# Wide rows for wo of heads 12 and 13, b1 in 16 rows, w2 in four pieces, early clearing of semaphores and sixteen more matmuls in a decode attention kernel

## The chip, the cores and the metric

The kernel runs on one core of a Trainium2 chip. The metric is the device time of one launch in microseconds. TensorE (PE) does matmuls into PSUM, VectorE (DVE) and ScalarE (ACT) do the rest of the arithmetic, GpSimd (POOL) makes one identity matrix, and SyncE (SP) issues almost all transfers. Transfers that SP issues stand in one queue that 16 transfer engines work off in order; ACT has a queue of its own for a few small loads and half of the stores.

## The reference

```
def _A_ref(x, k_cache, v_cache, wq, wo):            # B=2, H=16, Sk=4096, Dh=256, D=448
    q = (x @ wq).reshape(B, Sq, H, Dh).transpose(0, 2, 1, 3)
    scores = einsum("bhqd,bhkd->bhqk", q, k_cache) * (Dh ** -0.5)
    o = einsum("bhqk,bhkd->bhqd", softmax(scores), v_cache)
    return o.transpose(0, 2, 1, 3).reshape(B, Sq, H * Dh) @ wo
def _B_ref(x, w1, b1, w2, b2):                      # F=1792
    h = einsum("bsd,df->bsf", x, w1) + b1
    r = where(h > 0, h, 0)
    return einsum("bsf,fd->bsd", r * r, w2) + b2
g = sigmoid((x * gate_w).sum(-1, keepdims=True))
return g * A + (1 - g) * B                          # [2, 1, 448] float32
```

One query per batch row attends over 4096 cached keys; K and V are 134 MB each in float32, so nearly all of the kernel is reading them once.

## The kernel before

The work goes in 16 rounds (`rounds`): round i is one batch row and two heads. A round's K is 8192 KB, two heads on the 128 partitions, 64 partitions for each head, and so is its V. K goes by turns into the buffers `kp[0]` and `kp[1]`; V goes into `vp`, that of round 14 into `kp[0]`. DVE multiplies half a K by q (L412) and sums each row (L417), twice a round; PE turns the maxima over partitions (`maximum`, L427), ACT takes the exponentials (`softmax`, L435), and PE multiplies them with V (`values`, L479). A matmul is two PE instructions in float32, and four matmuls of different column groups run side by side.

Rounds 0 to 11 run on PE as a loop, the rest is written out. Heads are grouped in units: three of four heads (0 to 11), then 12, 13 and 14, 15. After each wide unit `turn_wide` turns the result so that it can be multiplied with wo, and `project` (L539) adds it to the sum `acc`. For the two last units `turn_narrow` (L518) and `late_wo` (L547) do the same on PSUM `fin`, four column quarters at a time; `late_w2` (L563) adds the second product of the feed-forward part to the same `fin`.

wo of a wide unit is loaded so that partition p holds 8 successive rows of wo, 14,336 bytes in one piece (`wo_g`, L531). For the last four heads it is loaded head by head, 3,584 bytes for each partition and head (`wo_v`, L530, in `load_wo`, L533). w2 goes into the first 6272 columns of `kp[1]` in five pieces with the borders `W2_CUTS` (L198), the V of the last round in three pieces with the borders `V_CUTS`.

Nothing plans the order: every engine does its operations in the order in which the code calls them, and waits on semaphores that `Flow` (L24) works out from what each reads and writes. On SP the last issues are: V of round 14, wo, the three pieces of V of round 15 (they wait for PE to be done with `vp`), five pieces of w2 (they wait for DVE to have summed the first half of `kp[1]`), a store of the unfinished result, and the last store. `store` (L638) writes half of the output from SP and half from ACT. At the end SP waits for both stores and then clears all semaphores (L171 to L174).

At the start ACT issues x, gate_w, b2 and b1; b1 goes straight into its final layout, 128 partitions with 14 numbers each (L305). It is used once, in `ffn_square` (L579). PE multiplies x with wq (L398), then with w1.

Of the kernel before, what the change touches and what calls it, by code (L numbers as in the profile page):

```python
# [6 lines left out]
AF = mybir.ActivationFunctionType  # L7
ALU = mybir.AluOpType
# [15 lines left out]
class Flow:  # L24
# [7 lines left out]
    def __init__(self, nc):  # L32
        self.nc = nc
        self.eng = {PE: nc.tensor, ACT: nc.scalar, DVE: nc.vector, POOL: nc.gpsimd, SP: nc.sync}
        self.order = {e: [] for e in self.eng}
        self.ops = {}
        self.know = {e: {} for e in self.eng}
        self.seen = {}
        self.tokens = {}
        self.parts, self.part, self.at = None, None, 0  # L40

    @staticmethod
    def span(r):
# [77 lines left out]
    def emit(self):  # L121
        nc = self.nc
        sems = {}
        counts = {}
        for proc, ops in self.ops.items():
            at = 0
            for o in ops:
                if proc not in self.eng:
                    o.inc = not o.give
                if o.inc and not o.give:  # L130
                    at += 1 if proc in self.eng else 16
                counts[id(o)] = at
        assert all(not t for t in self.tokens.values())

        def sem(name):
            if name not in sems:
                sems[name] = nc.alloc_semaphore(f"s_{name}")
            return sems[name]

        for proc in self.ops:  # L140
            sem(proc)
        for t in self.tokens:
            sem(t)

        def one(o):
# [12 lines left out]
        for eng in (POOL, DVE, ACT, SP, PE):  # L158
            for o in self.order[eng]:
                if isinstance(o, Op):  # L160
                    one(o)
                else:
                    outer, inner, body, rest, slot = o
                    engines = bass.OrderedEngineSet([TYPES[PE]])
                    with nc.Fori(0, outer, engines=engines, head_slot={TYPES[PE]: slot}):
                        with nc.Fori(0, inner, engines=engines):
                            for p in body:
                                one(p)
                        for p in rest:
                            one(p)  # L170
            if eng == SP:  # L171
                nums = sorted(s.num for s in sems.values())
                assert nums == list(range(nums[0], nums[0] + len(nums)))
                nc.sync.sem_clear(range(nums[0], nums[0] + len(nums)))  # L174


def gated_mix_kernel(nc, x, k_cache, v_cache, wq, wo, w1, b1, w2, b2, gate_w, out):
# [32 lines left out]
    def sb(name, *shape):  # L210
        return nc.alloc_sbuf_tensor(name, shape, F32).ap()
# [12 lines left out]
    rs_t = [sb(f"rs{n}", P, B * HG) for n in range(2)]  # L224
    eo = sb("eo", P, 2)
    m16 = sb("m16", P, 4 * HG)
    m8 = sb("m8", P, 2 * HG)
    rw = sb("rw", P, 2 * HG)
    o_t = sb("o", P, DH)
# [19 lines left out]
    oTn = [sb(f"oTn{n}", P, NJ, 2 * B) for n in range(2)]  # L249

    po_t = [bank(f"po{n}") for n in range(2)]
    acc = bank("acc")
# [9 lines left out]
    def load(eng, sem, dst, src, w, r=(), give=None):  # L262
        e = flow.eng[eng]
        op(eng, lambda: e.dma_start(dst, src), r=r, w=w, dma=sem, give=give)  # L264
# [32 lines left out]
    def at_start(k, n=1):  # L297
        return place(kp[1], k * D, (k + n) * D)
# [17 lines left out]
    def vec(fn, r, w, give=None):  # L316
        op(DVE, fn, r=r, w=w, give=give)
# [11 lines left out]
    vec(lambda: v_.tensor_reduce(m16, ident.rearrange("p (r k) -> p k r", r=4)[:, :4 * HG, :], axis=AX.X, op=ALU.add),  # L329
        ["ident"], ["m16"])  # L330
    vec(lambda: v_.tensor_reduce(m8, m16.rearrange("p (c s) -> p c s", s=2), axis=AX.X, op=ALU.add), ["m16"], ["m8"])

    xr = start_at[:, 4 * D:].rearrange("b (k r s) -> b k r s", k=XC, s=2)
    for s in range(2):
# [6 lines left out]
    def mms(calls):  # L341
        def run():
            for out_, lhsT, rhs, start, stop in calls:
                i = t_.matmul(out_, lhsT, rhs, start=start, stop=stop, skip_group_check=True)  # L344
            return i
        return run
# [158 lines left out]
    def turn_wide(u):  # L505
# [7 lines left out]
        for k in range(HG):  # L513
            at = slice(k * HP, (k + 1) * HP)
            op(ACT, lambda k=k, at=at: s_.activation(oTw[at], ptv[at, :, B * k:B * k + B], AF.Copy), r=["sm"], w=[("oTw", k, k + 1)],
               give="oT" if k == HG - 1 else None)

    def turn_narrow(u, between=lambda: None):  # L518
        ptv = sm[:, :NJ * 2 * B].rearrange("p (j c) -> p j c", c=2 * B)
        a = u - NG + 1  # L520
        po, name, rl, oT = po_t[u % 2], f"po{u % 2}", rl_t[u % 2], oTn[a]
        o = shared[:, a * 512:(a + 1) * 512]
        op(ACT, lambda: s_.activation(o, po, AF.Copy), r=[name], w=[("shared", a * 512, (a + 1) * 512)])  # L523
        between()
        ov = o.rearrange("r (s p j) -> r s j p", s=2, j=NJ)
        op(PE, mms([(ptv[:, j, :], ov[:, s, j, :], rl[:, :2 * B, s], s == 0, s == 1) for j in range(NJ) for s in range(2)]),
           r=[("shared", a * 512, (a + 1) * 512), f"rl{u % 2}"], w=["sm"])
        op(ACT, lambda: s_.activation(oT, ptv, AF.Copy), r=["sm"], w=[f"oTn{a}"])  # L528

    wo_v = wo.rearrange("(h p j) n -> p h (j n)", p=P, j=NJ)  # L530
    wo_g = wo.rearrange("(g p j) n -> g p (j n)", p=P, j=HJ)  # L531

    def load_wo(u):  # L533
# [12 lines left out]

    def late_wo(h):  # L547
        u, k = unit_of[h]
        t = wo_t.rearrange("p (h j n) -> p h j n", h=HG, j=NJ)
        calls = []  # L550
        for j in range(NJ):
            calls += late(oTn[u - NG + 1][:, j, B * k:B * k + B], t[:, h % HG, j, :])
        op(PE, mms(calls), r=[f"oTn{u - NG + 1}", "wo"], w=["fin"])
# [97 lines left out]
    softmax(i + 1)  # L651
    times_q(i + 2, 0, LEAD, J)
    values(i, vt)
    turn_narrow(NG - 1)
# [28 lines left out]
    vec(lambda: v_.tensor_copy(y4, fin[:, :DQ]), ["fin"], [("shared", 0, DQ)])  # L683
    store(y4, ("shared", 0, DQ))
    op(SP, lambda: nc.sync.nop(), r=["out0", "out1"])
    flow.emit()


# [24 lines left out]
```

## Time and profile before

| | us |
|---|---|
| median of 3 runs (lowest, highest) | 678.0 (677.81, 679.03) |
| the profiled execution's own time | 677.88 |
| its span, first to last instruction | 676.6 |
| PE, DVE, ACT busy | 259.4, 577.0, 49.5 |
| HBM read | 289.56 MB |
| mean granted TensorE clock | 0.649 |

The span is cut into 40 slices of 16.9 us in the page's timeline; a digit is a busy share in tenths. In the chain of waits a row is start, time and what the chain ran on; in the timeline it is start, time, engine, line and operation, with the idle time before it and what ended that in brackets. A row of issues ends with the time from issue to landing.

### The profile page before, as it was taken

Reading aid. Unit: us, or ns where it says so; the run is one execution under the profiler, and the core shown is the slowest. Engines: PE = TensorE matmul, PEld = TensorE weight load, DVE = VectorE, ACT = ScalarE, POOL = GpSimd, SP = SyncE. Lnnn points to the kernel's source line nnn. Section 1 sums busy time; section 2 is a strip of 40 time slices with the busy share of each in tenths; the row PEclk is TensorE's granted clock in tenths of the full one; section 3 lists DMA queues with packets and bytes.
Section 4 is the critical chain, followed back from the end, with each engine's and each line's share of the span. In section 5 each row is a group of like instructions: output and inputs, shape, how many; then the busy total and the mean of one; then the engine's idle time right before and its main releaser. Section 6 shows DMA issues by size and latency. Waiting matters only on the chain.

```text
span 676.6 us, 3524 instructions
## 1 busy us (share of the span) xinstructions
PE 259.4 (38%) x1518; PEld 84.0 (12%) x1518; DVE 577.0 (85%) x166; ACT 49.5 (7%) x151; POOL 0.7 (0%) x6
## 2 busy tenths in 40 slices
PE   2622151512305662150515356051421563512487
PEld 1100010100101310010101311010100133100123
DVE  3069999999999896989989896998989899999940
ACT  0100101010000301010010301001010120000000
POOL 0000000000000000000000000000000000000000
PEclk9957585655658576585756577575665775575888
DMA  9999999999999999999999999999999999999997
GB/s 381 434 430 435 434 434 434 434 434 434 434 434 434 446 434 434 434 430 430 434 434 426 457 434 434 434 434 434 434 430 434 396 465 430 434 434 434 390 437 292
DMA packets 7059, 289.66 MB, mean 428 GB/s; under 512 B 902, under 2 KB 1036, under 8 KB 1932
## 3 DMA queue, kind: packets, MB, share of 16 engines
q1 hardware_dynamic: 6880, 289.54, 99.2%
q8 instruction: 5, 0.08, 0.0%
q10 hardware_dynamic: 172, 0.02, 0.0%
q14 instruction: 2, 0.02, 0.0%
HBM read 289.56 MB, written 0.01 MB: 428 GB/s over the span
## 4 chain that ended last, share of the span: by engine, by line
DMA 42%; DVE 26%; PE 4%; issue 0%; ACT 0%; SPq 0%
DMA kp<-in_A_k_cache_dram 26%; DMA vp<-in_A_v_cache_dram 16%; DVE s L417 13%; DVE kp L412 13%; PE po L344 4%; PE fin L344 0%; PE sm L344 0%; PE mt L344 0%; SPq L264 0%; ACT shared L523 0%; DVE nb L440 0%; DVE shared L683 0%; ACT oTn L528 0%
## 5 line engine op out<-in xcount | busy, mean ns | idle before, releaser
L412 DVE TENSOR_TENSOR kp<-kp,q 128x8192 f32<-128x8192 f32 (+2 forms) x34 | 278.3, 8184 | 48.1 <-DMA kp<-in_A_k_cache_dram 47.9
L417 DVE TENSOR_REDUCE s<-kp 128x32 f32<-128x8192 f32 x32 | 277.9, 8686 | 1.1
L344 PE MATMUL po<-vp,pw 128*16 128x512 f32 (+1 forms) x960 | 141.1, 753 | 216.1 <-PEq L148 195.9
L344 PEld LDWEIGHTS po<-vp,pw 128*16 128x16 f32 (+1 forms) x960 | 32.1, 113 | 328.9 <-issue 307.2
L344 PE MATMUL mt<-ident,m 128*128 128x128 f32 x32 | 11.8, 468 | 139.9 <-PEq L148 90.5
L459 ACT ACTIVATE pw<-zero 128x128 f32<-128x128 f32 x12 | 3.7, 312 | 317.1 <-PE po L344 317.1
L344 PEld LDWEIGHTS mt<-ident,m 128*128 128x128 f32 x32 | 7.6, 295 | 153.3 <-issue 101.2
L344 PE MATMUL acc<-wo,oTw 128*2 128x448 f32 x48 | 25.2, 694 | 3.2 <-PEq L148 3.2
L448 ACT ACTIVATE pw<-s,nb 64x64 f32<-64x64 f32 x32 | 11.1, 348 | 193.5 <-DVE nb L440 193.3
L344 PE MATMUL pq<-qs,sel 128*128 128x512 f32 x24 | 22.4, 1036 | 0.0
L440 DVE TENSOR_REDUCE nb<-mt 64x1 f32<-64x64 f32 x32 | 7.1, 221 | 13.1 <-PE mt L344 12.6
L683 DVE COPY shared<-fin 128x112 f32<-128x112 f32 x1 | 0.3, 275 | 19.9 <-PE fin L344 19.9
L344 PE MATMUL sm<-rw,shared 128*128 128x8 f32 x48 | 10.7, 360 | 11.5 <-PEq L148 11.5
L392 ACT ACTIVATE q<-pq 64x256 f32<-64x256 f32 x32 | 12.1, 379 | 24.8 <-PE pq L344 24.5
L344 PE MATMUL ph<-vp,xT 128*4 128x448 f32 x28 | 8.3, 765 | 14.2 <-DMA vp<-in_B_w_dram 14.2
L344 PE MATMUL po<-kp,pw 128*8 128x512 f32 x64 | 9.6, 754 | 8.7 <-DMA kp<-in_A_v_cache_dram 8.7
L344 PEld LDWEIGHTS sm<-rw,shared 128*128 128x128 f32 x48 | 10.5, 330 | 11.7 <-issue 11.7
L344 PE MATMUL po<-vp,xT 128*4 128x512 f32 x56 | 8.8, 798 | 4.7 <-DMA vp<-in_A_wq_dram 4.7
L344 PE MATMUL sm<-ident,wo 4*128 4x4 f32 x28 | 7.0, 380 | 1.9 <-ACT wo L572 1.9
L344 PEld LDWEIGHTS acc<-wo,oTw 128*2 128x2 f32 x48 | 4.6, 100 | 21.6 <-issue 21.6
L344 PEld LDWEIGHTS sm<-ident,wo 4*128 4x128 f32 x28 | 6.9, 336 | 2.8 <-ACT wo L572 2.8
L507 ACT ACTIVATE shared<-o 128x1024 f32<-128x1024 f32 x3 | 6.3, 2101 | 2.6 <-DVE o L503 2.6
(76 smaller groups left out, 79.6 us busy)
## 6 DMA issues: line engine op xcount, KB each, us to landing
vp<-in_A_wq_dram SPq DMA_DIRECT2D x1, 7168.0 KB, 19.4
wo<-in_A_wo_dram SPq DMA_DIRECT2D x4, 1792.0 KB, 44.6
vp<-in_A_v_cache_dram SPq DMA_DIRECT2D x1, 4096.0 KB, 24.7
vp<-in_B_w_dram SPq DMA_DIRECT2D x1, 3136.0 KB, 17.9
vp<-in_A_v_cache_dram SPq DMA_DIRECT2D x1, 3072.0 KB, 31.6
kp<-in_B_w_dram SPq DMA_DIRECT2D x1, 1344.0 KB, 37.1
vp<-in_A_v_cache_dram SPq DMA_DIRECT2D x1, 1024.0 KB, 33.7
kp<-in_B_w_dram SPq DMA_DIRECT2D x2, 448.0 KB, 33.5
```

The source lines that it names most:

```text
L344: i = t_.matmul(out_, lhsT, rhs, start=start, stop=stop, skip_group_check=True)
L392: op(ACT, lambda k=k, at=at: s_.activation(t[at], pq[at, k * DH:(k + 1) * DH], AF.Copy), r=["pq"], w=[(f"q{i % 3}", k, k + 1)])
L412: vec(lambda: v_.tensor_tensor(kt, kt, q.unsqueeze(1).to_broadcast([P, hi - lo, DH]), op=ALU.mult), at + [f"q{i % 3}"], at)
L417: vec(lambda: v_.tensor_reduce(s[:, at], rows(t)[:, at, :], axis=AX.X, op=ALU.add), [place(t, half * HALF, (half + 1) * HALF)], [(f"s{i % ...
L440: vec(lambda at=at: v_.tensor_reduce(nb[at], mt[at, at], axis=AX.X, op=ALU.max, negate=True), ["mt"], [(f"nb{i % 2}", at.start, at.stop)])
L448: op(ACT, lambda: s_.activation(pw[at, :, 2 * c:2 * c + 2], s[at].rearrange("p (m s) -> p m s", s=2), AF.Exp, bias=nb[at], accum_out=rs[at ...
L459: op(ACT, lambda: s_.activation(at, zero.unsqueeze(2).unsqueeze(3).to_broadcast([P, NK // 2, 2, 2]), AF.Copy), r=["zero"], w=[("pw0", 2 * ...
L507: op(ACT, lambda: s_.activation(o_w, o_t.rearrange("r (p j) -> r j p", j=HJ).unsqueeze(2).to_broadcast([P, HJ, HG, HP]), AF.Copy), r=["o"] ...
L683: vec(lambda: v_.tensor_copy(y4, fin[:, :DQ]), ["fin"], [("shared", 0, DQ)])
```

## The change

- **wo of heads 12 to 15.** `load_wo(NG - 1)` loads heads 12 and 13 alone, in wide rows, into partitions 0 to 63 of the wo tile. `turn_half` is new: it turns unit 3 as `turn_wide` turns the wide ones, two ACT copies, 16 matmuls, two ACT copies into `oT2` of 64 partitions; `late_half` multiplies with 32 matmuls. `load_wo(NG)` loads heads 14 and 15 in the old rows, into free columns of `kp[1]` behind w2; `late_wo` reads them there.
- **b1.** It is loaded as 16 rows of 112 numbers. A matmul with a 16-row selection matrix `e16` spreads each row to 8 partitions, a multiplication with the mask `m_i` and a sum pick the 14 numbers of each partition. All of it lies in `kp[1]` before K of round 1 is loaded there.
- **w2.** The pieces 0 to 2 and 2 to 8 become one.
- **Order on PE.** The first two chunks of w2 are no longer multiplied during the last turn, but after it with the rest.
- **Matmuls in waits.** `keep_busy` multiplies a matrix of ones with data that lie in `kp[0]`, into PSUM `ph`, which nobody reads any more: 6 before the first piece of the last V, 10 after it.
- **Semaphores.** ACT reports when it has issued its last store; SP then clears all semaphores but those of the two stores, waits for these, and sets each back by subtraction.

```diff
-    W2_CUTS = (2, 8, 11, 13)
+    W2_CUTS = (8, 11, 13)
+    BUSY = (6, 10)
...
-    load(ACT, "b1", b1T, b1.rearrange("(p c) -> p c", c=FC), ["b1T"])
+    load(ACT, "b1", b1r, b1.rearrange("(r n) -> r n", r=BR), [b1r_at])
...
+    op(PE, mms([(ph[:, :BI * FC], e16, b1r, True, True)]), r=[e16_at, b1r_at], w=["ph"])
+    vec(lambda: v_.tensor_tensor(b1w.rearrange("p (c i) -> p c i", i=BI), ph[:, :BI * FC].rearrange("p (i c) -> p c i", i=BI),
+                                 m_i.unsqueeze(1).to_broadcast([P, FC, BI]), op=ALU.mult), ["ph", "m_i"], [b1w_at])
+    vec(lambda: v_.tensor_reduce(b1T, b1w.rearrange("p (c i) -> p c i", i=BI), axis=AX.X, op=ALU.add), [b1w_at], ["b1T"])
...
+    def turn_half():
+        u = NG - 1
+        ptv = sm[:PH, :HJ * 2 * B].rearrange("p (j c) -> p j c", c=2 * B)
...
+        op(PE, mms([(ptv[:, j, :], ov[:, s, j, :], rl[:, :2 * B, s], s == 0, s == 1) for j in range(HJ) for s in range(2)]),
+           r=["shared", f"rl{u % 2}"], w=["sm"])
...
+        elif u < NG:
+            load(SP, "wo", wo_t[:PH], wo_g[u, :PH], ["wo"])
         else:
-            load(SP, "wo", wo_t.rearrange("p (h k) -> p h k", h=HG), wo_v[:, u * HG:(u + 1) * HG, :], ["wo"])
+            load(SP, "wo_e", wo_e.rearrange("p h j n -> p h (j n)"), wo_v[:, H - 2:, :], [wo_e_at])
...
+    def keep_busy(n):
+        op(PE, mms([(ph[32 * (k % 4):32 * (k % 4) + 16, :], ones_pp[:, :16], kp[0][:, :2 * DH], True, True) for k in range(n)]),
+           r=["ones", place(kp[0], 0, 2 * DH)], w=["ph"])
...
+    def late_half():
+        t = wo_t[:PH].rearrange("p (j n) -> p j n", j=HJ)
+        calls = []
+        for j in range(HJ):
+            calls += late(oT2[:, j, :], t[:, j, :])
+        op(PE, mms(calls), r=["oT2", "wo"], w=["fin"])
...
     load_wo(NG - 1)
+    load_wo(NG)
     vt_next = load_v(i + 1, vp, V_CUTS)
...
-    late_wo(H - 4)
-    late_wo(H - 3)
+    late_half()
     sums(NG)
     norm(NG)
+    keep_busy(BUSY[0])
...
         values(last, vt, lo, hi)
-    turn_narrow(NG, lambda: late_w2(0, W2_CUTS[0]))
-    late_wo(H - 2)
-    late_wo(H - 1)
-    late_w2(W2_CUTS[0], FC)
+        if lo == 0:
+            keep_busy(BUSY[1])
+    turn_narrow(NG)
+    late_wo(0)
+    late_wo(1)
+    late_w2(0, FC)
...
+            if eng == ACT:
+                nc.scalar.nop().then_inc(sem("acted"), 1)
             if eng == SP:
-                nums = sorted(s.num for s in sems.values())
-                assert nums == list(range(nums[0], nums[0] + len(nums)))
-                nc.sync.sem_clear(range(nums[0], nums[0] + len(nums)))
+                nc.sync.wait_ge(sem("acted"), 1)
+                nc.sync.sem_clear(range(inner[0], inner[0] + len(inner)))
+                for proc in ends:
+                    n = 16 * len(self.ops[proc])
+                    nc.sync.wait_ge(sem(proc), n).then_inc(sem(proc), -n)
```

The order of issues on SP, from V of round 14 on (a row is line, operation, destination and source, the destination's shape, and the semaphores waited for), before:

```order
L264 DMA kp0<-in_A_v_cache_dram 128x16384 [waits s_DVE]
L264 DMA wo<-in_A_wo_dram 128x4x896
L264 DMA vp<-in_A_v_cache_dram 128x8192 [waits s_PE]
L264 DMA vp<-in_A_v_cache_dram 128x6144
L264 DMA vp<-in_A_v_cache_dram 128x2048
L264 DMA kp1<-in_B_w2_dram 128x896 [waits s_DVE]
L264 DMA kp1<-in_B_w2_dram 128x2688
```

and after:

```order
L279 DMA kp0<-in_A_v_cache_dram 128x16384 [waits s_DVE]
L279 DMA wo<-in_A_wo_dram 64x3584
L279 DMA kp1<-in_A_wo_dram 128x2x896 [waits s_DVE]
L279 DMA vp<-in_A_v_cache_dram 128x8192 [waits s_PE]
L279 DMA vp<-in_A_v_cache_dram 128x6144
L279 DMA vp<-in_A_v_cache_dram 128x2048
L279 DMA kp1<-in_B_w2_dram 128x3584
```

wo is two loads, the first onto 64 partitions; the wait for DVE moved from w2's first piece to wo's second, ahead of the last V.

The last part of PE's order, from the product of heads 12 and 13 with wo on (x15 is a count of rows alike), before:

```order
L344 MATMUL fin<-wo,oTn0 2x112 [waits s_wo,s_ACT,s_DVE]
L344 MATMUL fin<-wo,oTn0 2x112 x15
L344 MATMUL sm<-rs0,ones_pp 128x4 [waits s_ACT]
L344 MATMUL po0<-vp,pw1 8x512 [waits s_v15_0]
L344 MATMUL po0<-vp,pw1 8x512 x15
L344 MATMUL po0<-vp,pw1 8x512 [waits s_v15_32]
L344 MATMUL po0<-vp,pw1 8x512 x11
L344 MATMUL po0<-vp,pw1 8x512 [waits s_v15_56]
L344 MATMUL po0<-vp,pw1 8x512 x3
L344 MATMUL fin<-kp1,hT 2x112 [waits s_w2_0]
L344 MATMUL fin<-kp1,hT 2x112 x7
L344 MATMUL sm<-rl0,shared 128x4 [waits s_ACT,s_DVE]
```

and after:

```order
L372 MATMUL fin<-wo,oT2 2x112 [waits s_wo,s_ACT,s_DVE]
L372 MATMUL fin<-wo,oT2 2x112 x31
L372 MATMUL sm<-rs0,ones_pp 128x4 [waits s_ACT]
L372 MATMUL ph<-kp0,ones_pp 16x512 x6
L372 MATMUL po0<-vp,pw1 8x512 [waits s_v15_0]
L372 MATMUL po0<-vp,pw1 8x512 x15
L372 MATMUL ph<-kp0,ones_pp 16x512 x10
L372 MATMUL po0<-vp,pw1 8x512 [waits s_v15_32]
L372 MATMUL po0<-vp,pw1 8x512 x11
L372 MATMUL po0<-vp,pw1 8x512 [waits s_v15_56]
L372 MATMUL po0<-vp,pw1 8x512 x3
L372 MATMUL sm<-rl0,shared 128x4 [waits s_ACT,s_DVE]
```

The 6 and the 10 added matmuls stand on either side of the first piece's values, the product with wo is twice as long, and w2's first eight matmuls no longer stand ahead of the turn.

More of the change, by code (lines that the diff above doesn't have):

```diff
@@ L40, in __init__ @@
         self.parts, self.part, self.at = None, None, 0
+        self.last = ("out0", "out1")
     @staticmethod
@@ L138, in sem @@
             return sems[name]
+        ends = [p for p in self.ops if p in self.last]
         for proc in self.ops:
-            sem(proc)
+            if proc not in ends:
+                sem(proc)
         for t in self.tokens:
             sem(t)
+        sem("acted")
+        inner = sorted(s.num for s in sems.values())
+        assert inner == list(range(inner[0], inner[0] + len(inner)))
+        for proc in ends:
+            sem(proc)
         def one(o):
@@ L226, in gated_mix_kernel @@
     m16 = sb("m16", P, 4 * HG)
+    m_i = sb("m_i", P, 8)
     m8 = sb("m8", P, 2 * HG)
@@ L248, in gated_mix_kernel @@
     oTw = sb("oTw", P, HJ, B)
-    oTn = [sb(f"oTn{n}", P, NJ, 2 * B) for n in range(2)]
+    oT2 = sb("oT2", P // 2, HJ, B)
+    oTn = sb("oTn", P, NJ, 2 * B)
     po_t = [bank(f"po{n}") for n in range(2)]
@@ L304, in gated_mix_kernel @@
     load(ACT, "b2", b2r, b2[None, :].to_broadcast([B, D]), [at_start(2)])
-    load(ACT, "b1", b1T, b1.rearrange("(p c) -> p c", c=FC), ["b1T"])
+    BR = 16
+    BI = P // BR
+    b1_at = 4 * D + XC * P
+    b1r = kp[1][:BR, b1_at:b1_at + BI * FC]
+    e16 = kp[1][:BR, b1_at + BI * FC:b1_at + BI * FC + P]
+    b1w = kp[1][:, b1_at + BI * FC + P:b1_at + 2 * BI * FC + P]
+    b1r_at = place(kp[1], b1_at, b1_at + BI * FC)
+    e16_at = place(kp[1], b1_at + BI * FC, b1_at + BI * FC + P)
+    b1w_at = place(kp[1], b1_at + BI * FC + P, b1_at + 2 * BI * FC + P)
+    load(ACT, "b1", b1r, b1.rearrange("(r n) -> r n", r=BR), [b1r_at])
     v_, s_, t_, g_ = nc.vector, nc.scalar, nc.tensor, nc.gpsimd
@@ L516, in turn_wide @@
                give="oT" if k == HG - 1 else None)
+    def turn_half():
+        u = NG - 1
+        ptv = sm[:PH, :HJ * 2 * B].rearrange("p (j c) -> p j c", c=2 * B)
+        po, rl = po_t[u % 2], rl_t[u % 2]
+        o_h = shared.rearrange("r (s j k p) -> r s j k p", s=2, j=HJ, k=2)
+        pv = po.rearrange("r (s p j) -> r s j p", s=2, j=HJ)
+        for s in range(2):
+            op(ACT, lambda s=s: s_.activation(o_h[:, s], pv[:, s].unsqueeze(2).to_broadcast([P, HJ, 2, HP]), AF.Copy),
+               r=[f"po{u % 2}"], w=[("shared", s * HN // 2, (s + 1) * HN // 2)])
+        ov = o_h.rearrange("r s j k p -> r s j (k p)")
+        op(PE, mms([(ptv[:, j, :], ov[:, s, j, :], rl[:, :2 * B, s], s == 0, s == 1) for j in range(HJ) for s in range(2)]),
+           r=["shared", f"rl{u % 2}"], w=["sm"])
+        for k in range(2):
+            at = slice(k * HP, (k + 1) * HP)
+            op(ACT, lambda k=k, at=at: s_.activation(oT2[at], ptv[at, :, B * k:B * k + B], AF.Copy), r=["sm"], w=[("oT2", k, k + 1)])
     def turn_narrow(u, between=lambda: None):
         ptv = sm[:, :NJ * 2 * B].rearrange("p (j c) -> p j c", c=2 * B)
[L520 to L523, printed above, removed]
+        po, name, rl = po_t[u % 2], f"po{u % 2}", rl_t[u % 2]
+        o = shared[:, 512:1024]
+        op(ACT, lambda: s_.activation(o, po, AF.Copy), r=[name], w=[("shared", 512, 1024)])
         between()
@@ L526, in turn_narrow @@
         op(PE, mms([(ptv[:, j, :], ov[:, s, j, :], rl[:, :2 * B, s], s == 0, s == 1) for j in range(NJ) for s in range(2)]),
-           r=[("shared", a * 512, (a + 1) * 512), f"rl{u % 2}"], w=["sm"])
-        op(ACT, lambda: s_.activation(oT, ptv, AF.Copy), r=["sm"], w=[f"oTn{a}"])
+           r=[("shared", 512, 1024), f"rl{u % 2}"], w=["sm"])
+        op(ACT, lambda: s_.activation(oTn, ptv, AF.Copy), r=["sm"], w=["oTn"])
     wo_v = wo.rearrange("(h p j) n -> p h (j n)", p=P, j=NJ)
     wo_g = wo.rearrange("(g p j) n -> g p (j n)", p=P, j=HJ)
+    wo_e = kp[last % 2][:, FC * D:FC * D + 2 * NJ * D].rearrange("p (h j n) -> p h j n", h=2, j=NJ)
+    wo_e_at = place(kp[last % 2], FC * D, FC * D + 2 * NJ * D)
+    assert FC * D + 2 * NJ * D <= HALF
     def load_wo(u):
@@ L653, in gated_mix_kernel @@
     values(i, vt)
-    turn_narrow(NG - 1)
+    turn_half()
     i = last - 1
@@ L684, in gated_mix_kernel @@
     store(y4, ("shared", 0, DQ))
-    op(SP, lambda: nc.sync.nop(), r=["out0", "out1"])
     flow.emit()
```

12 lines of the change are left out of this document (7 added, 5 removed).

## The prediction

> **What bounds the kernel now.** I read the page's time slices and queues first, then the chain of waits in order of time for the last 85 us.
>
> ```profile
> DMA  9999999999999999999999999999999999999997
> GB/s 381 434 430 435 434 434 434 434 434 434 434 434 434 446 434 434 434 430 430 434 434 426 457 434 434 434 434 434 434 430 434 396 465 430 434 434 434 390 437 292
> q1 hardware_dynamic: 6880, 289.54, 99.2%
> ```
>
> The transfer engines are busy in every slice, at 434 GB/s, and the one queue that SP feeds fills 99.2% of them. Everything else has spare time; an edit that makes the queue longer by a microsecond makes the kernel longer by a microsecond, and an edit elsewhere counts only after the last transfer. So the end matters next:
>
> ```profile
> 631.81 31.63 DMA vp<-in_A_v_cache_dram
> 663.49 5.36 PE po L344 x32
> ...
> 670.96 3.29 PE fin L344 x128
> 674.27 0.28 DVE shared L683
> ```
>
> After the second piece of the last V (663.49) the chain names no DMA: PE runs through values, turn, wo and w2 to 674.27. But it runs very close to the queue. The next rows are SP's issues (start, time) and, for single transfers, the microseconds from issue to landing.
>
> ```profile
> 612.32 0.33 SPq L264 DMA_DIRECT2D kp<-in_A_v_cache_dram  x1
> 612.69 0.43 SPq L264 DMA_DIRECT2D wo<-in_A_wo_dram  x1
> 632.76 0.43 SPq L264 DMA_DIRECT2D kp<-in_B_w_dram  x1
> 633.24 6.00 SPq L264 DMA_DIRECT2D kp<-in_B_w_dram  x1
> 641.39 1.06 SPq L264 DMA_DIRECT2D kp<-in_B_w_dram  x1
> kp<-in_A_v_cache_dram SPq DMA_DIRECT2D x1, 29.6
> wo<-in_A_wo_dram SPq DMA_DIRECT2D x1, 1792.0 KB, 33.7
> kp<-in_B_w_dram SPq DMA_DIRECT2D x1, 448.0 KB, 34.3
> kp<-in_B_w_dram SPq DMA_DIRECT2D x1, 1344.0 KB, 37.1
> kp<-in_B_w_dram SPq DMA_DIRECT2D x1, 224.0 KB, 32.2
> 671.72 2.48 PE L344 MATMUL fin<-kp,hT 128*2 128x112 f32 x96
> ```
>
> The last piece of w2 lands at 641.39 + 32.2 = 673.6. PE's last 96 matmuls begin at 671.72, one each 24 ns or so, so the eight that need this piece begin about 671.72 + 88 x 0.024 = 673.83. **PE is 0.24 us behind the queue.** A faster PE can win 0.2 us and no more; a longer queue costs nearly all of its length.
>
> **wo of heads 12 to 15.** It was one transfer of 1792 KB in rows of 3,584 bytes. Now half of it (heads 12, 13) goes in rows of 14,336 bytes into partitions 0 to 63, and half (heads 14, 15) in the old short rows into kp1. Old price: landing of wo minus landing of the V before it, (612.69 + 33.7) - (612.32 + 29.6) = 4.5 us. For wide rows the loop's wo is the nearest row, as large, with the same 14,336 bytes per partition but on 128 partitions:
>
> ```profile
> 497.92 0.33 SPq L264 DMA_DIRECT2D kp<-in_A_k_cache_dram  x1
> 498.29 0.43 SPq L264 DMA_DIRECT2D wo<-in_A_wo_dram  x1
> kp<-in_A_k_cache_dram SPq DMA_DIRECT2D x1, 42.6
> wo<-in_A_wo_dram SPq DMA_DIRECT2D x1, 1792.0 KB, 46.6
> ```
>
> (498.29 + 46.6) - (497.92 + 42.6) = 4.4 us. No transfer of any size in this trace goes to 64 partitions, so the new one is bounded from both sides. If time goes by bytes, it takes half, 2.2 us; with 2.2 us for the narrow half that is 4.4, a gain of 0.1. If time goes by bytes per partition, it takes the full 4.4 us, 6.6 in all, a loss of 2.1. I take the upper end. The 434 GB/s hold alike for K, V and w2, whatever the row length and wherever the source lies, so the ceiling is in what all loads share; all of them write 128 partitions evenly, and half the partitions would then offer half the ceiling. The trace does not prove it: sixteen engines at their own limit would look the same. [...]
>
> The issue itself hides nothing and delays nothing. The new short-row load waits for DVE's row sums over kp1's first half, done before SP's V pieces at 631.43 are free to go, and the queue is then full to 646.4.
>
> **w2 in four pieces.** 448 and 1344 KB become one load of 1792 KB with rows of 14,336 bytes. The second landed (633.24 + 37.1) - (632.76 + 34.3) = 3.3 us after the first, 2.4 ns per KB, so the pair takes 4.4 us, against 4.4 for the wide wo of the same size. Gain 0 to 0.1, taken 0.05. SP's 6.00 us in one issue may go with fewer rows; the transfer it issues lands 31 us later, so that is hidden.
>
> **b1 in 16 rows.** 128 writes of 56 bytes become 16 of 448, plus one matmul and four small DVE operations.
>
> ```profile
> q10 hardware_dynamic: 172, 0.02, 0.0%
> 9.40 0.61 DVE L365 SCALAR_TENSOR_TENSOR kp<-kp 2x448 f32<-2x448 f32 x1 [2.12 <-DMA kp<-in_gate_w_dram]
> 13.81 1.65 PE L344 MATMUL acc<-kp,gd 2*2 2x448 f32 x2 [2.48 <-DMA kp<-in_B_b_dram]
> 20.20 8.80 PE L344 MATMUL po<-vp,xT 128*4 128x512 f32 x56 [4.74 <-DMA vp<-in_A_wq_dram]
> 39.63 8.69 DVE L412 TENSOR_TENSOR kp<-kp,q 128x8192 f32<-128x8192 f32 x1 [28.10 <-DMA kp<-in_A_k_cache_dram]
> ```
>
> ACT's queue prints as 0.0% of the span, so all of it is under 0.3 us: gain 0 to 0.3, taken 0.05, since the packets are a few bytes each. The new wait: PE now needs b1 before it starts wq's product, and K1's load waits for DVE's last b1 step. gate_w and b2 are waited for until 9.4 and 13.8, 4.4 us apart, so b1 comes near 18.2, two microseconds before wq at 20.2. Were it late, DVE's first product waits for K at 39.6 anyway, and the queue holds K until then: cost 0 until b1 is some 6 us late.
>
> **Matmuls in PE's waits.** The granted clock decides how fast V's last pieces go. Rows of the windows: window, its length, PE busy (count), weight loads, DVE, ACT, POOL, clock, DMA share, GB/s.
>
> ```profile
> 653.56:656.97 3.41, 1.01 (x10) 0.37 (x14) 0.51 (x3) 0.00 (x0) 0.00 (x0) 1.00 1.00 423
> 656.97:660.39 3.42, 3.42 (x20) 0.71 (x16) 0.00 (x0) 0.00 (x0) 0.00 (x0) 0.50 1.02 438
> 660.39:663.80 3.41, 1.43 (x16) 0.23 (x12) 0.00 (x0) 0.00 (x0) 0.00 (x0) 1.00 0.89 372
> 663.80:667.21 3.41, 3.41 (x20) 0.71 (x16) 0.00 (x0) 0.00 (x0) 0.00 (x0) 0.50 1.05 435
> 649.09 3.62 PE L344 MATMUL po<-kp,pw 128*8 128x512 f32 x32
> 656.19 5.32 PE L344 MATMUL po<-vp,pw 128*8 128x512 f32 x32 [2.40 <-DMA vp<-in_A_v_cache_dram]
> 663.49 5.32 PE L344 MATMUL po<-vp,pw 128*8 128x512 f32 x32 [1.98 <-DMA vp<-in_A_v_cache_dram]
> 641.95 5.97 PE L344 MATMUL po<-kp,pw 128*8 128x512 f32 x32 [8.69 <-DMA kp<-in_A_v_cache_dram]
> ```
>
> A window with PE busy 1.0 or 1.4 of 3.4 us is followed by one at half clock, a full one by full clock; 32 instructions take 3.62 us at full clock and 5.32 when part of them is at half. [...]
>
> A matmul is two instructions, so the added 6 are 12 x 0.113 = 1.4 us (2.8 at half clock), the 10 are 2.3 us (4.5). Heads 12 and 13 now also need 32 more PE instructions of 25 ns, 0.8 us, in the first wait. 0.8 + 1.4 = 2.2 us fits into 2.40; V's first piece is not held up, and comes 2 us later if wo does. The first values then end 1.7 us sooner, so the second wait is 3.7 us, of which 2.3 are filled. The clock should stay up; the last values end 1.7 us sooner too. (V's last piece, in the queue ahead of w2's first 448 KB, lands near 667.06 - 1.1 = 666.0 and needs 8 instructions, so it does not bind.) Against that, the eight matmuls of w2's first piece that ran during the turn, 16 instructions of 24 ns, 0.4 us, now come behind it. PE is 1.3 us ahead of where it was and waits for w2 piece by piece. Gain 0.2, bounded by the 0.24; lower end 0.
>
> The wider turn (16 matmuls for 4, three microseconds more) lies in the 8.69 us wait. More PE instructions may bring one more load of program text, 16 KB on one transfer engine (434 / 16 = 27 GB/s, 0.6 us), which counts only on the engine that ends last: 0 to 0.6, taken 0.05.
>
> ```profile
> q8 instruction: 5, 0.08, 0.0%
> 674.57 0.51 SPq L264 DMA_DIRECT2D out_dram<-shared  x1
> SPq L685 <- DMA out_dram<-shared: 1.3, 1, 1.3
> ```
>
> **Early clearing.** The last store is seen at 674.57 + 0.51 + 1.3 = 676.4, the span ends at 676.6. Of these 0.2 us the clear goes and two waits with their own subtraction stay: gain 0 to 0.15, taken 0.1. Each other engine has finished.
>
> **Sum**, on the profiled execution's own 677.88 us (span 676.6 and 1.3 around it; the median of three is 678.0, 0.1 above): +2.1 wo, -0.05 w2, -0.05 b1, -0.2 PE, +0.05 program text, -0.1 clear = +1.75, **679.6 us**.
>
> **Rivals.** *The 64-row load goes by bytes.* For it: rows of 3.5 to 64 KB all reach the same rate, so sixteen engines may be the only limit; against it, no row has fewer than 128 partitions. wo then gains 0.1: -0.1 - 0.05 - 0.05 - 0.2 + 0.05 - 0.1 = -0.45, 677.4. It decides from the point where that load lands under 2.6 us after V. *The added matmuls don't hold the clock* (a gap of 1.4 us meets a window badly) and the load goes by bytes: w2's eight matmuls now come after the turn, PE ends 0.2 later than before, the clear gives 0.1 back: 678.0. *Forecast plus a program load on the last engine:* +0.6, 680.2. *One of the edits removes a cost that no row shows:* 676.4, for it only that 0.9% of the queue is unaccounted.
>
> **Chances.** Forecast 0.60, own range 679.1 to 680.1; by bytes 0.27; clock lost 0.04; program load 0.05; unseen gain 0.04. About 0.2% (1.4 us, to 679.4 or 676.6) is what a measurement of this kernel can tell from no change. Slower: 0.46 of the forecast's 0.60, and 0.05, is 0.51. Faster: 0.04 and 0.02 of by bytes, 0.06. Within: the rest, 0.43. The range runs from 677.2 to 680.1.
>
> **What would show it.** wo's first part landing 4.4 us after V rather than 2.2; the last w2 piece near 675.5; PE waiting for it; full clock from 650 to the end; the span ending within 0.1 us of the last store. A wo that lands in 2.2 us makes the prediction wrong by its largest term.

## The result, and the profile after

The changed kernel takes 683.32 us (median of 6 runs, 682.86 to 683.84) against 677.96 for the kernel before (677.81 to 679.03): a ratio of 1.0075, 95% interval 1.0063 to 1.0088. It is slower by 5.4 us. The forecast was 679.6, with a range up to 680.1: the sign is right, the size is not. The profiled execution took 683.52 us with a span of 682.2, 5.6 above the profiled execution of before.

The page of the kernel after: bandwidth by slice (17.06 us each), and the queues that carry the loads and the program text.

```profile
GB/s 378 469 427 443 434 434 427 430 434 430 430 431 408 441 430 442 446 438 438 434 430 434 423 430 430 430 430 430 434 430 430 461 431 434 434 430 428 277 416 294
q1 hardware_dynamic: 6560, 289.54, 99.2%
q8 instruction: 6, 0.10, 0.1%
```

The queue carries the same 289.54 MB and is as full as before. But one slice, the third from the end (631 to 648 us), moves 277 GB/s where its neighbours move 428 and 416. Rows of windows show where, before:

```profile
639.50:645.50 6.00, 3.55 (x20) 0.75 (x24) 5.96 (x2) 0.00 (x0) 0.00 (x0) 0.50 1.03 416
```

and after (the last three columns are clock, DMA share, GB/s):

```profile
639.50:645.50 6.00, 0.00 (x0) 0.00 (x0) 5.96 (x2) 0.00 (x0) 0.00 (x0) 0.50 0.82 127
```

By their share (0.82) the transfer engines are still busy most of the time, but they move less than a third of what they moved. SP's issues of V of round 14, of the two parts of wo, and of w2, with the time from issue to landing for the three single ones, after:

```profile
612.76 0.33 SPq L279 DMA_DIRECT2D kp<-in_A_v_cache_dram  x1
613.13 0.58 SPq L279 DMA_DIRECT2D wo<-in_A_wo_dram  x1
631.50 0.39 SPq L279 DMA_DIRECT2D kp<-in_A_wo_dram  x1
633.40 1.85 SPq L279 DMA_DIRECT2D kp<-in_B_w_dram  x4
...
kp<-in_A_v_cache_dram SPq DMA_DIRECT2D x1, 33.3
...
wo<-in_A_wo_dram SPq DMA_DIRECT2D x1, 896.0 KB, 37.3
...
kp<-in_A_wo_dram SPq DMA_DIRECT2D x1, 896.0 KB, 20.9
```

Landings are issue plus landing time. V: 612.76 + 33.3 = 646.1. Wide part of wo: 613.13 + 37.3 = 650.4. Narrow part: 631.50 + 20.9 = 652.4. Before, by the rows in the prediction, V landed at 641.9 and the whole of wo at 646.4. So the loss of 6.0 us comes, up to rounding, in three steps: **V, which lies ahead of the new load and was not touched, is 4.1 us later**; the 64-row load takes 4.4 us behind V where its bytes need 2.2, 2.2 more; the narrow part takes 2.0, 0.2 less.

From there the delay runs to the end. PE, its weight loads (PEld) and DVE in the timeline, after:

```profile
662.19 3.62 PE L372 MATMUL po<-vp,pw 128*8 128x512 f32 x32 [2.83 <-DMA vp<-in_A_v_cache_dram]
...
669.52 3.62 PE L372 MATMUL po<-vp,pw 128*8 128x512 f32 x32 [1.15 <-DMA vp<-in_A_v_cache_dram]
...
676.29 1.45 PEld L372 LDWEIGHTS fin<-kp,hT 128*2 128x2 f32 x64 [0.32 <-DMA kp<-in_B_w_dram]
677.92 0.49 PEld L372 LDWEIGHTS fin<-kp,hT 128*2 128x2 f32 x24 [0.18 <-DMA kp<-in_B_w_dram]
679.01 0.30 PEld L372 LDWEIGHTS fin<-kp,hT 128*2 128x2 f32 x16 [0.60 <-DMA kp<-in_B_w_dram]
679.56 0.11 PEld L372 LDWEIGHTS fin<-kp,hT 128*2 128x2 f32 x8 [0.26 <-DMA kp<-in_B_w_dram]
680.00 0.28 DVE L748 COPY shared<-fin 128x112 f32<-128x112 f32 x1 [21.85 <-PE fin L372]
```

PE waits four times for w2, piece by piece, and the last piece lets it go at 679.56, 5.9 us after the 673.6 of before. The final copy starts 0.44 us behind that (before, 0.67 behind the landing). The values of the last V take 3.62 us twice, not 5.32.

### The profile page after: what moved, and what is told of

Read it like the earlier page. It is cut to its first block, busy times and chain, and to the rows that moved or that the text cites. A ratio compares the mean times of both kernels' runs of the same rounds, so it can differ in the third digit from the quotient of the medians.

```text
span 682.2 us, 3714 instructions
## 1 busy us (share of the span) xinstructions
PE 259.0 (38%) x1608; PEld 84.8 (12%) x1608; DVE 577.9 (85%) x170; ACT 50.1 (7%) x153; POOL 0.7 (0%) x6
## 3 DMA queue, kind: packets, MB, share of 16 engines
q1 hardware_dynamic: 6560, 289.54, 99.2%
## 5 line engine op out<-in xcount | busy, mean ns | idle before, releaser
L372 PE MATMUL po<-vp,pw 128*16 128x512 f32 (+1 forms) x960 | 133.4, 717 | 217.4 <-PEq L156 198.0
L372 PEld LDWEIGHTS po<-vp,pw 128*16 128x16 f32 (+1 forms) x960 | 30.4, 109 | 325.1 <-issue 302.6
## 6 DMA issues: line engine op xcount, KB each, us to landing
wo<-in_A_wo_dram SPq DMA_DIRECT2D x1, 896.0 KB, 37.3
```

## The experiments

Each ran beside the kernel before on the same chip; ratios are to that one. The kernel before took 677.83 us beside the first four, 678.04 beside the next four, 677.88 beside the two whose wo comes in 7,168-byte rows and the two with one load at the queue's end, and 678.16 beside the last three. The runs with short rows, with two quarters, with 64 rows at the queue's end and with a second neighbour behind them have two executions each, the others three to twelve.

**One part undone: wo as before, all other edits kept.**

```diff
...
-            load(SP, "wo", wo_t[:PH], wo_g[u, :PH], ["wo"])
-            load(SP, "wo_e", wo_e.rearrange("p h j n -> p h (j n)"), wo_v[:, H - 2:, :], [wo_e_at])
+            load(SP, "wo", wo_t.rearrange("p (h k) -> p h k", h=HG), wo_v[:, u * HG:(u + 1) * HG, :], ["wo"])
...
-    turn_half()
+    turn_narrow(NG - 1)
...
-    late_half()
+    late_wo(H - 4)
+    late_wo(H - 3)
...
```

> The changed kernel with wo of heads 12 to 15 loaded and multiplied as before (one load, rows of 3,584 bytes, 128 partitions); b1, w2, the matmuls in the waits, the order on PE and the early clear stay. Theory 'half the partitions' (the load onto partitions 0 to 63 costs the whole loss): 677.2 to 677.7, that is the gains of the other edits, 0.2 to 0.8 under the kernel before. Rival 'another edit' (the split of wo, b1's wait, the matmuls or the clear cost it): 681 or more.

Measured: 678.03 us against 677.83, ratio 1.0001 [0.9992, 1.0011]. The whole loss is gone, so it sits in the wo edit. The forecast's other terms, -0.35 together, don't show: the time lies above the 677.2 to 677.7 expected, though the interval (-0.5 to +0.7 us) would hold them.

**That part alone: the kernel before with nothing but the new wo** (the same lines, added to the kernel before).

> The kernel before with only the change of wo (heads 12 and 13 in 64 wide rows, heads 14 and 15 in kp1, the wider turn). Theory 'half the partitions': 683.5 to 684.5, slower than the whole change, whose other edits win about half a microsecond. Rival 'another edit': 677.5 to 679.

Measured: 683.17, ratio 1.0074 [1.0059, 1.0089]. The wo edit alone gives the whole loss. It is 0.3 us under the range expected, where the other edits were to have made the difference.

**All 128 partitions, wide rows, twice the bytes.**

```diff
-            load(SP, "wo", wo_t[:PH], wo_g[u, :PH], ["wo"])
+            load(SP, "wo", wo_t, wo_g[u], ["wo"])
```

> The changed kernel, but the first wo load brings 128 wide rows instead of 64, twice the bytes (wo of heads 14 and 15 comes twice, and the wide copy isn't used). Theory 'half the partitions': the load takes 4.4 us as in the loop and nothing near it is slowed, 679.3 to 680, faster than the change by some 3.7 although it reads 0.9 MB more. Rival 'it is the split into two loads': 683 or more; rival 'by bytes': 685.

Measured: 680.59, ratio 1.0040 [1.0026, 1.0053]. It reads 896 KB more than the changed kernel and is 2.7 us faster. Of its 2.8 us over the kernel before, 2.2 are the added bytes, at half the price of the loop's wo (4.4 us). The rest, which puts the time above the 679.3 to 680 expected, fits the end of the profiled execution, where the last products with w2 took 4.38 us, against 3.6 at full clock, waits included, in the run with 7,168-byte rows below:

```profile
672.63 4.38 PE L372 MATMUL fin<-kp,hT 128*2 128x112 f32 x112
```

So wide rows by themselves are not what costs; that leaves the number of partitions, or which they are.

**The same 64 rows, on every second partition.** PE still reads partitions 0 to 63, so the part of heads 12 and 13 in the output is not the reference's.

```diff
-            load(SP, "wo", wo_t[:PH], wo_g[u, :PH], ["wo"])
+            load(SP, "wo", wo_t[::2], wo_g[u, :PH], ["wo"])
```

> The changed kernel with the same 64 wide rows written to partitions 0, 2, 4 to 126 instead of 0 to 63; the product still reads partitions 0 to 63, so the output lacks the right values of heads 12 and 13. If it matters where the 64 partitions lie (a crowd on the lower half), the load takes 2.2 to 3 us and the kernel 677.3 to 678.5. If it matters that there are only 64 rows, 4 for each transfer engine, it stays at 683.

Measured: 677.80, ratio 1.0001 [0.9991, 1.0011]. The same window, in this kernel:

```profile
639.50:645.50 6.00, 3.19 (x16) 0.59 (x20) 5.97 (x2) 0.00 (x0) 0.00 (x0) 0.50 1.02 423
```

With the same 64 rows of 14,336 bytes spread out, 423 GB/s move in this window. Here not the number of partitions counts, but which ones.

**The upper half: partitions 64 to 127.**

```diff
-            load(SP, "wo", wo_t[:PH], wo_g[u, :PH], ["wo"])
+            load(SP, "wo", wo_t[PH:], wo_g[u, :PH], ["wo"])
```

Here too PE reads partitions 0 to 63, and the part of heads 12 and 13 is not the reference's.

> The changed kernel with the 64 wide rows written to partitions 64 to 127; the product still reads 0 to 63, so the values of heads 12 and 13 aren't those of the reference. If any crowd on one half costs the same: 683 to 684. If the lower half has something of its own: 677.5 to 680.

Measured: 683.43, ratio 1.0090 [1.0069, 1.0111]; in the profiled execution, the fastest of four (682.00 to 685.17), the window moves 173 GB/s:

```profile
639.50:645.50 6.00, 1.13 (x8) 0.28 (x12) 5.96 (x2) 0.00 (x0) 0.00 (x0) 0.50 0.88 173
```

The lower half is nothing special.

**Shorter rows into the same 64 partitions.**

```diff
-            load(SP, "wo", wo_t[:PH], wo_g[u, :PH], ["wo"])
+            load(SP, "wo", wo_t[:PH].rearrange("p (a k) -> p a k", a=4), wo_g[u, :PH].rearrange("p (a k) -> p a k", a=4), ["wo"])
```

> The changed kernel with the 64 rows still on partitions 0 to 63, but each brought in four pieces of 3,584 bytes. If the price comes from where the bytes land: 683 to 684. If it comes from long rows that block one another: 679.5 to 681.

Measured: 683.15, ratio 1.0075 [1.0046, 1.0105]. On rows this run tells nothing: its page counts the same 6560 packets on the queue as the changed kernel's, so no shorter row was moved. That makes it a repeat of the changed kernel, and one thing in its trace differs, the first values of the last V:

```profile
662.08 5.32 PE L372 MATMUL po<-vp,pw 128*8 128x512 f32 x32 [2.67 <-DMA vp<-in_A_v_cache_dram]
```

They took 5.32 us with the added matmuls in place, as in the kernel before, whose 5.32 us had a mean granted clock of 0.68.

**Two quarters, one in each half: 32 rows to partitions 0 to 31, 32 to 64 to 95.** Heads 12 and 13 are again not the reference's.

```diff
-            load(SP, "wo", wo_t[:PH], wo_g[u, :PH], ["wo"])
+            load(SP, "wo", wo_t[:32], wo_g[u, :32], [("wo", 0, 32)])
+            load(SP, "wo_b", wo_t[64:96], wo_g[u, 32:PH], [("wo", 32, 64)])
```

> The changed kernel with two loads of 32 wide rows, one to partitions 0 to 31, one to 64 to 95; the product reads 0 to 63, so heads 12 and 13 lack the reference's values. If only the balance of bytes between the halves counts: 677.5 to 678.5, no loss. If it is a crowd of all sixteen engines on few partitions at one moment: as slow as the change, 683 or more.

Measured: 683.04, ratio 1.0074 [1.0044, 1.0103]. An even share for both halves over two loads does not help. That it fails because at any one moment most engines write to one half fits, but no trace here shows which engine writes where.

**Half the rows: 32 rows to partitions 0 to 31.** The wo of head 13 is left out.

```diff
-            load(SP, "wo", wo_t[:PH], wo_g[u, :PH], ["wo"])
+            load(SP, "wo", wo_t[:32], wo_g[u, :32], ["wo"])
```

> The changed kernel with only 32 of the 64 wide rows loaded, to partitions 0 to 31 (head 13's wo is left out, half a megabyte less). Without any loss that would be 676.7. A price by bytes on the half: 2.9 more, 679.6. A crowd that is twice as dense on 32 partitions: nearly the whole loss again, 681.5 to 682.7.

Measured: 680.15, ratio 1.0031 [1.0020, 1.0042]. Its 448 KB fewer are worth 1.1 us at 434 GB/s, so it loses 2.1 + 1.1 = 3.2 us (2.4 to 3.9 by the interval); the change loses 5.4. Half the bytes lose about half, as a price by bytes on the half says, and not nearly the whole, as a twice as dense crowd would.

**A form that should win: 7,168-byte rows on all 128 partitions.** The heads lie four rows of wo to a partition; the turn takes 8 matmuls and the product 16.

```diff
...
-            load(SP, "wo", wo_t[:PH], wo_g[u, :PH], ["wo"])
+            load(SP, "wo", wo_t[:, :HJ // 2 * D], wo[u * HN:u * HN + 2 * DH].rearrange("(p j) n -> p (j n)", p=P), ["wo"])
...
-        t = wo_t[:PH].rearrange("p (j n) -> p j n", j=HJ)
+        t = wo_t[:, :HJ // 2 * D].rearrange("p (j n) -> p j n", j=HJ // 2)
...
```

> The changed kernel, but heads 12 and 13 of wo come in 7,168-byte rows on all 128 partitions, four rows of wo to a partition, instead of 14,336-byte rows on 64; the same 896 KB. Theory (the whole loss is the crowd of the transfer engines on few partitions): wo lands some 2.2 us after V, as its half did before; nothing of the 5.4 is lost; the fewer V matmuls in the last turn and the held clock are kept: 677.3 to 677.8. Rival (it is row length or the wide form itself that costs): 680 or more. The run with wo as before gave 678.03, so that 677.9 to 678.1 would say that the rest of the change brings nothing that can be measured.

Measured: 678.44, ratio 1.0008 [0.9999, 1.0017]. Issues and landings of V and wo, this kernel:

```profile
612.85 0.33 SPq L279 DMA_DIRECT2D kp<-in_A_v_cache_dram  x1
613.22 0.43 SPq L279 DMA_DIRECT2D wo<-in_A_wo_dram  x1
...
wo<-in_A_wo_dram SPq DMA_DIRECT2D x1, 896.0 KB, 31.1
...
kp<-in_A_v_cache_dram SPq DMA_DIRECT2D x1, 29.3
```

wo lands at 644.3, 2.2 us behind V at 642.1. The loss is gone, as expected; the gain expected on top (677.3 to 677.8) is not there. No version tried beats the kernel before by more than the noise.

**The same without the sixteen matmuls.**

```diff
-    keep_busy(BUSY[0])
...
-        if lo == 0:
-            keep_busy(BUSY[1])
```

> The kernel of x_best_128_rows without the sixteen added matmuls in PE's waits. If they hold the clock and the clock matters at the end: the granted clock falls to about half in the stretch behind the first idle gap over 2 us, PE's last turns take longer, 0.1 to 0.4 us above x_best_128_rows. If the end is set by the transfers alone: the same within 0.1 us.

Measured: 678.42, ratio 1.0008 [0.9999, 1.0018]: no difference in time. In the trace there is one. Values of the last V and two windows of this kernel:

```profile
656.39 5.32 PE L372 MATMUL po<-vp,pw 128*8 128x512 f32 x32 [2.57 <-DMA vp<-in_A_v_cache_dram]
...
656.50:660.00 3.50, 3.50 (x20) 0.71 (x17) 0.00 (x0) 0.00 (x0) 0.00 (x0) 0.52 1.00 428
670.10:673.50 3.40, 3.40 (x84) 2.47 (x76) 0.00 (x0) 0.00 (x0) 0.00 (x0) 0.51 0.51 195
674.89 0.28 DVE L746 COPY shared<-fin 128x112 f32<-128x112 f32 x1 [20.45 <-PE fin L372]
```

The clock is at half after a gap of 2.57 us and again at the end, and the final copy starts at 674.89. With the matmuls the first values took 3.62 us at full clock, and the copy starts here:

```profile
674.12 0.28 DVE L749 COPY shared<-fin 128x112 f32<-128x112 f32 x1 [19.19 <-PE fin L372]
```

But these 0.77 us are not shown to be the added matmuls' work. The slow first values cost next to nothing, since the second values wait for V in both, without the matmuls and with them:

```profile
663.70 3.62 PE L372 MATMUL po<-vp,pw 128*8 128x512 f32 x32 [1.99 <-DMA vp<-in_A_v_cache_dram]
663.62 3.62 PE L372 MATMUL po<-vp,pw 128*8 128x512 f32 x32 [1.12 <-DMA vp<-in_A_v_cache_dram]
```

From there on PE does the same in both. What sets the copy back is the second stretch at half clock, 670.10 to 673.50, and that does not go with the added matmuls: the run with 128 wide rows keeps them and takes 4.38 us for the last products with w2, against 3.6 at full clock with the wait for w2's last piece in it. The first values mostly do go with them: they took 3.62 us in three kernels that have the added matmuls (the changed one, the one with wo as before and the one with 7,168-byte rows), 5.32 in a fourth, the run with short rows, and 5.32 in two that lack them, this one and the kernel before. That is no gain in time, and over 11 and 12 runs the medians agree, as the expectation "the end is set by the transfers alone" says.

**The load by itself, at the queue's end.** The kernel before, with one load of 896 KB that nobody reads behind w2: on 64 partitions, and as a measure on 128.

```diff
     load_w2()
+    x_at = place(kp[last % 2], HALF, HALF + HJ * D)
+    load(SP, "extra", kp[last % 2][:PH, HALF:HALF + HJ * D], wo_g[0, :PH], [x_at])
...
-    op(SP, lambda: nc.sync.nop(), r=["out0", "out1"])
+    op(SP, lambda: nc.sync.nop(), r=["out0", "out1", x_at])
```

By the last line the kernel ends only when the extra load has landed; so it is with every load added below.

> The kernel before, with one load more at the end of the queue, 896 KB of wo into 64 partitions in 14,336-byte rows, that nobody reads; its landing behind w2's last piece is the price of the form by itself. If 64 contiguous partitions halve the rate and the neighbours made up the rest: 4.2 to 4.5 us behind w2's last piece (673.6), so at 678, and the kernel ends 1.5 to 2 us later than before (679.5). If the form itself runs at a third: 6 us or more, at 679.7 or later, and the kernel ends at 681 or later. Should w2's last piece land later than before by over 1 us, the neighbour ahead is slowed too.

> As x_tail_64, but the 896 KB come in 7,168-byte rows on 128 partitions. Both theories: 2.2 us behind w2's last piece, at 675.8, ahead of the last store's landing, so that the time is 677.9 to 678.3.

Measured: 681.85 on 64 partitions, ratio 1.0059 [1.0041, 1.0076]; 678.38 on 128, ratio 1.0007 [0.9997, 1.0017]. Last piece of w2 (224 KB) and the extra load, on 64 partitions:

```profile
641.63 1.06 SPq L264 DMA_DIRECT2D kp<-in_B_w_dram  x1
648.45 0.57 SPq L264 DMA_DIRECT2D kp<-in_A_wo_dram  x1
...
kp<-in_A_wo_dram SPq DMA_DIRECT2D x1, 896.0 KB, 31.2
kp<-in_B_w_dram SPq DMA_DIRECT2D x1, 224.0 KB, 36.1
```

and on 128:

```profile
641.63 1.06 SPq L264 DMA_DIRECT2D kp<-in_B_w_dram  x1
648.38 0.33 SPq L264 DMA_DIRECT2D kp<-in_A_wo_dram  x1
...
kp<-in_A_wo_dram SPq DMA_DIRECT2D x1, 896.0 KB, 27.7
kp<-in_B_w_dram SPq DMA_DIRECT2D x1, 224.0 KB, 32.3
```

On 128 partitions w2 ends at 673.9 and the load at 676.1, 2.2 later. On 64, w2, which lies **ahead**, ends at 677.7, 3.8 late, and the load at 679.65, only 1.9 behind it. The loss at the landing is 3.6 us. The two theories said about 2 and about 4, so time and landing lie near the second, the form itself at a third of the rate; but the neighbour ahead is slowed too, and nearly all of the loss is seen there. This run can't tell the two apart.

**With a second neighbour behind it, and with none.** First, 896 KB on 128 partitions follow the 64-row load:

```diff
     load(SP, "extra", kp[last % 2][:PH, HALF:HALF + HJ * D], wo_g[0, :PH], [x_at])
+    y_at = place(kp[last % 2], HALF + HJ * D, HALF + HJ * D + HJ // 2 * D)
+    load(SP, "extra2", kp[last % 2][:, HALF + HJ * D:HALF + HJ * D + HJ // 2 * D], wo[:2 * DH].rearrange("(p j) n -> p (j n)", p=P), [y_at])
```

> As x_tail_64, with 896 KB more behind it in 7,168-byte rows on 128 partitions, which take 2.2 us by themselves. In x_tail_64 the 64-row load landed 6.1 us behind where w2 ended before (679.67 against 673.60), a loss of 3.9; in the changed kernel, where another load follows it, the loss is 5.9. If the loss of 3.9 is all and the rest comes from what lies ahead: the second load lands 2.2 behind the first, at 681.9. If the load behind is slowed too while the transfer engines that are ahead begin it beside the crowd: the 64-row load itself lands later than 679.67 by some 2 us, and the second load lands near 683.7 to 684.

Then the 64-row load, or the 128-row one, after the last matmul, on an idle queue:

```diff
     store(y4, ("shared", 0, DQ))
+    x_at = place(kp[last % 2], 0, HJ * D)
+    load(SP, "extra", kp[last % 2][:PH, :HJ * D], wo_g[0, :PH], [x_at])
```

> The kernel before, and after the last matmul, with nothing else on the queue but the store of 1.8 KB, one load of 896 KB of wo into 64 partitions in 14,336-byte rows. The price of the form with no neighbour: 4.2 us or less of transfer where neighbours made the rest (2 us above x_alone_128); 6 us (4 us above x_alone_128) where the form itself runs at a third.

> As x_alone_64, with the 896 KB in 7,168-byte rows on 128 partitions: 2.2 us of transfer behind the time that an issue takes to begin, the measure for x_alone_64.

Measured with a neighbour behind: 685.34, ratio 1.0106 [1.0062, 1.0149]. The two loads, each with its landing time:

```profile
648.39 0.57 SPq L264 DMA_DIRECT2D kp<-in_A_wo_dram  x1
...
kp<-in_A_wo_dram SPq DMA_DIRECT2D x1, 896.0 KB, 33.7
...
649.01 5.25 SPq L264 DMA_DIRECT2D kp<-in_A_wo_dram  x1
...
kp<-in_A_wo_dram SPq DMA_DIRECT2D x1, 896.0 KB, 35.0
```

The 64-row load now lands at 682.1, 2.4 later than with nothing behind it, and the other at 684.0. Both landings are where the second theory, "the load behind is slowed too", had them. On 128 partitions both would end at an estimated 676.1 + 2.2 = 678.3, so the loss is 5.7 us, about the size that the changed kernel shows. Measured alone: 683.65 on 64 partitions and 681.84 on 128, a difference of 1.8. Issue and landing on 64:

```profile
675.15 0.54 SPq L264 DMA_DIRECT2D kp<-in_A_wo_dram  x1
...
kp<-in_A_wo_dram SPq DMA_DIRECT2D x1, 896.0 KB, 7.2
```

and on 128:

```profile
675.05 0.44 SPq L264 DMA_DIRECT2D kp<-in_A_wo_dram  x1
...
kp<-in_A_wo_dram SPq DMA_DIRECT2D x1, 896.0 KB, 5.0
```

Alone, 64 partitions cost 2.2 us more. Against the 2.2 us that the 128-row load takes in a full queue that is an estimate of 4.4 us of transfer, half the rate. The theory that the form itself runs at a third, 4 us more, falls. **The loss is 2.2 us alone, 3.6 with a transfer ahead, 5.7 with transfers ahead and behind**, each from the landings of single executions.

## Why the prediction was wrong

**wo, the term that failed.** The step reads: "If time goes by bytes per partition, it takes the full 4.4 us, 6.6 in all, a loss of 2.1. I take the upper end." The mechanism and the load's own price were right where the load runs alone: 2.2 us lost. The term was mis-sized, +2.1 for a measured +6.0, because the load was priced as if it had the queue to itself: V ahead of it was taken to land when it did before, and landed 4.1 us later. The upper end of the bound came from a row of one load's bytes per partition, and no bound was put on what the load does to its neighbours. The transfer engines don't work in step: the sixteen parts of V of round 14 ended between 639.90 and 641.90 in the trace of before, which has a report for each, 2.0 us from the first to the last. In the changed kernel the parts of the same V ended between 639.90 and 646.07, and the first part of wo landed at 645.82, ahead of the last of V. Ten of V's sixteen parts were in by 640.76 (by 640.34 before), so it is the last six that are held up; that the engines done early hold them up by writing wo fits, but is not shown. That the neighbour shares the crowd is also shown by the w2 piece that came 3.8 us late with nothing of its own changed. Why a crowd with neighbours moves 127 GB/s, and not the half estimated for the load alone, was not settled.

The sign that the prediction named for its mechanism, wo 4.4 us behind V, came true in part by luck. V was itself late, and at the queue's end the same load landed only 1.9 us behind w2 while 3.6 were lost: beside neighbours the distance of two landings is not the load's price.

That half of the partitions gives half the rate was an estimate of the author's, since no load in the trace of before goes to 64 of them. What the runs show is that the place counts: 2.2 us lost alone on partitions 0 to 63 (7.2 us from issue to landing against 5.0 on 128), nothing lost on every second partition (677.80 us against 677.83), and in the full queue of the changed kernel about three times the 2.1 of the term. Why the place counts, no trace here shows.

**The other terms.** Their sum was -0.35. The run with wo as before gave 678.03 against 677.83, so over many runs nothing of them can be told from zero. In the profiled executions +5.9 at w2's last landing became +5.6 in span. Of the 0.3 between them, 0.1 fits the early clearing: the span ends 2.2 us after the final copy's start in the changed kernel and 2.3 in the kernel before. The other 0.2 looks like the -0.2 of the faster PE, since the copy starts 0.44 us behind the last piece of w2 instead of 0.67, but it isn't shown to be. In the run that loads 64 rows alone, PE's program up to that copy is the one of before:

```profile
673.85 0.11 PEld L344 LDWEIGHTS fin<-kp,hT 128*2 128x2 f32 x8 [0.25 <-DMA kp<-in_B_w_dram]
674.30 0.28 DVE L683 COPY shared<-fin 128x112 f32<-128x112 f32 x1 [19.85 <-PE fin L344]
```

Here the old PE waits for w2's last piece, and the copy starts 0.45 us behind it. So the "0.24 us behind the queue", on which the -0.2 rested, belonged to one execution of the kernel before and not to the kernel.

- *Clock:* it was held, but not by the rule that the prediction read. The granted clock from the second-last V's values to the end, after:

```profile
649.95:680.00 30.05, 24.54 (x364) 9.60 (x356) 1.24 (x6) 1.65 (x6) 0.00 (x0) 1.00 0.90 381
660.19:663.60 3.41, 1.41 (x16) 0.44 (x20) 0.00 (x0) 0.00 (x0) 0.00 (x0) 1.00 0.98 420
663.60:667.02 3.42, 3.42 (x40) 0.89 (x30) 0.00 (x0) 0.00 (x0) 0.00 (x0) 1.00 0.93 393
```

  Before, a window with PE busy 1.43 of 3.41 us was followed by half clock (0.50); here one with 1.41 was followed by full clock (1.00), behind a gap of 2.83 us. The repeat with short rows took 5.32 us instead of 3.62 after 2.67 us at the same place. So part of this is luck, and what decides stays open. Without the added matmuls a gap of 2.57 us was followed by a clock of 0.52.
- *b1:* right. PE's product for b1 and the one that it might have delayed, after:

```profile
18.30 0.76 PE L372 MATMUL ph<-kp 16*128 16x112 f32 x2 [2.63 <-DMA kp<-in_B_b_dram]
20.42 1.04 PE L372 MATMUL po<-vp,xT 128*4 128x512 f32 x4 [1.35 <-DMA vp<-in_A_wq_dram]
```

  b1 came at 18.3 (forecast 18.2), and PE then still waited 1.35 us for wq.
- *w2 and SP's long issue:* the issue of 6.00 us is gone here, four issues take 1.85, and that was hidden, as said. It does not go with the number of pieces: the run with wo as before loads w2 in the same four and spends 7.68 us on them. A gain of 0.05 is below what can be seen.
- *Program text:* one more load, 6 for 5, as said; its price was not separated.

**The rivals.** "The 64-row load goes by bytes" falls by the load alone, 2.2 us slower on 64 partitions than on 128. With it falls "the clock is lost", which took the load to go by bytes; "an unseen gain" (the page's 99.2% leave 0.8% of the queue for it, not 0.9) falls by the sign, and a program load at its estimated 0.6 us would have left most of the loss unexplained. The missing case was the forecast's own mechanism with a wider reach; the range ended where the load's own price ended, at 680.1, just under the 680.2 of one of its own rivals.

## What to carry to other kernels

A load onto half of the partitions in one block cost more than its own lost bandwidth when the queue was full: bound it with the transfers ahead and behind, here about two and a half times the price alone (5.4 to 5.7 us against 2.2). Spread the same bytes over all 128 partitions, in shorter rows if need be; that cost nothing here that could be told from noise (678.44 us against 677.88). And before spending edits on PE in a kernel whose queue is full to the end, look at more than one execution: the 0.2 us that PE lagged in one were not there in another, and faster first values of V showed in the trace and not in the time.

## What had not been expected

- A transfer was slowed by one that is *behind* it in the same queue: V by 4.1 us, w2's last piece by 3.8.
- The same 64 rows cost 5.4 us on partitions 0 to 63 and nothing on 0, 2, 4 to 126 (677.80 us against 677.83).
- Splitting the load over both halves in turn, 32 partitions each, lost as much (ratio 1.0074); an even share over two loads was not enough.
